# Key-value products on column halves: keys and values of an attention pair in blocks of 128 successive tokens

## The chip, the cores and the metric

The kernel runs on one core of a Trainium2 chip. The metric is the device time of one execution in microseconds (us); lower is better. All data are float32.

## The reference

Performer attention (random features in place of the softmax over keys) is followed by an FNet block (a Fourier transform as the mixer, then an MLP). There are 8 batches of 8 heads, 576 tokens, head dimension 64 and 128 random features.

```python
def phi(x):                                   # x = q or k, times 64**-0.25
    proj = np.einsum('bhsd,md->bhsm', x, omega)
    h = proj - np.sum(x * x, -1, keepdims=True) / 2
    h = h - np.max(h, -1, keepdims=True)
    return np.exp(h) / np.sqrt(m)
kv  = np.einsum('bhsm,bhsd->bhmd', phi(k), v)  # a sum over the tokens s
z   = np.sum(phi(k), axis=2)
num = np.einsum('bhsm,bhmd->bhsd', phi(q), kv)
den = np.einsum('bhsm,bhm->bhs', phi(q), z)[..., None] + 1e-6
x   = (num / den), heads side by side: (8, 576, 512)
mixed = real(fft(fft(x, tokens), channels)); u = x + mixed
un = layer_norm(u); out = u + relu(un @ w_ch1) @ w_ch2
```

The sums `kv` and `z` run over all tokens of a head, so the order of the tokens in them is free, as long as keys and values have the same one.

## The kernel before

A *pair* is two heads of one batch; there are 32 of them. The 1152 tokens of a pair (head 0's 576, then head 1's) lie on 128 partitions in R = 9 blocks. Before the change, partition p of each half of the tile holds the nine successive tokens 9p to 9p + 8 of one head, so in every block the partitions 0 to 63 are head 0 and 64 to 127 head 1.

`loads` fetches k and q of a pair into one tile `kq` (two buffers; lines L471 and L474), `load_v` the values into one of three tiles `vd` (L479), where each block has 64 columns of v and a 65th of ones, which makes `z` come out beside `kv`. All of these are issued by SP's queue, in a fixed order with the loads of the weights, the tables and the stores.

`attn` then does, for each pair: transposes of `kq` on TensorE (L607) and their copies out of PSUM (L621, L623); projections onto the features (L701, for the first six pairs on row halves, 64*128, for the others on quarters of the array, 64*64); the maximum (L644) and the exponential (L661) of softmax into tiles `e`; the **key-value step** (L735), which sums features times values over the nine blocks into two PSUM banks `kvp`; a copy of it to `kv` (L749 on VectorE or L751 on ScalarE); transposes of the query features (L607 again); the numerator and denominator (L782 and L790) on column halves, 128*64; and the division (L799 to L811).

The key-value step has four quarters: head i is rows 64i to 64i + 63 of the array, feature half h is its columns 64h to 64h + 63. Each head sums into its own bank, `kvp[cols, i]`. Each of the nine blocks gives one matmul to each quarter, 36 in all.

Beside the attention run the Fourier transforms of the batches that are done (L894, L904, L944, L955), conversions of the weights on DVE, ACT and POOL (L532 to L550), and the first token tiles of the MLP (L1236, L1259). The second part, from about 375 us on, is the rest of the MLP (L1727, L1878, L2178).

The order of instructions on each engine is fixed. A planner (`Listing`) takes the `Step`s of all streams, with a cost for each, and the picks of an earlier search are written into the kernel as strings; so the order of the work on each engine does not depend on what the steps really cost. The tile framework puts in the waits.

Of the kernel before, what the change touches and what calls it, by code (L numbers as in the profile page):

```python
# [375 lines left out]
def kernel(  # L376
# [10 lines left out]
    nc = tc.nc  # L387

    B, H, S, D = q.shape
# [13 lines left out]
    P = 128  # L403

    R = S // 64

    NS = 3
    NV = 3
# [38 lines left out]
        kq=NKQ, turned=NS, e=NE, e1=NS, kv=NS, x0=1, x1=1, fold=1, half=1, y=1,  # L447
# [8 lines left out]
    def got():  # L456

        return listing.got, psum_of(listing.got)
# [2 lines left out]
    kqs = {}  # L461
    vds = []

    def loads():
        for n in range(B * NP):
            b, pr = divmod(n, NP)
            h = slice(2 * pr, 2 * pr + 2)
            rows = "i (p r) d -> (i p) r d"
            yield Step(SP, 0.37, 3.0, take=("kq",), makes=("k", n), kb=288)
            kq = ld.tile([P, 2 * R, D], F32, name="kq", tag="kq")  # L470
            nc.sync.dma_start(kq[:, 0:R, :], k[b, h].rearrange(rows, r=R))  # L471
            kqs[n] = kq
            yield Step(SP, 0.47, 3.6, makes=("kq", n), kb=288, bias=-2.98)
            nc.sync.dma_start(kq[:, R : 2 * R, :], q[b, h].rearrange(rows, r=R))  # L474

    def load_v(n):
        b, pr = divmod(n, NP)
        yield Step(SP, 0.63, 4.0, take=(f"vd{n % NV}",), makes=("vd", n), kb=500, bias=0.52)
        nc.sync.dma_start(  # L479
            vds[n % NV][:, :, 0:D],  # L480
            v[b, 2 * pr : 2 * pr + 2].rearrange("i (p r) d -> (i p) r d", r=R),
        )

    def loads_v():
        for n in range(B * NP):
            yield from load_v(n)
# [181 lines left out]
    def attn(n):  # L668
        b, pr = divmod(n, NP)

        yield Step(NONE, after=(("k", n),) + ((("vd", n - 1),) if n else ()))
        kq = kqs.pop(n)
# [40 lines left out]
        def place(c):  # L713
            if c in (R - 1, R):
                return 2, c - (R - 1)
            return (c % 2, c // 2) if c < R else (3 + c % 2, (c - R - 1) // 2)

        def feature(c):
            t, i = place(c)
            return es[t][:, i, :]  # L720
# [8 lines left out]
            give=("e", "e", f"vd{n % NV}"), bias=-0.19,  # L729
        )  # L730
        kvb, kvp = got()
        for r in range(R):
            for i, h in ((0, 0), (1, 1), (0, 1), (1, 0)):
                rows, cols = slice(D * i, D * i + D), slice(D * h, D * h + D)
                nc.tensor.matmul(  # L735
                    kvp[cols, i, 0 : D + 1],
                    lhsT=feature(r)[rows, cols],
                    rhs=vds[n % NV][rows, r, :],
                    start=(r == 0),
                    stop=(r == R - 1),  # L740
                )
        kvs = []

        def keep():
# [32 lines left out]
        for i in range(2):  # L777
            for c in range(4):
                half = int(c in (1, 2))
                for g in range(2):  # L780
# [3 lines left out]
                        lhsT=flat[:, c0 : c0 + D],  # L784
                        rhs=kvs[0][:, i, :],
                    )

        for i in range(2):
            for g in range(2):
                nc.tensor.matmul(  # L790
                    ndp[D * g : D * g + D, i, (D + 1) * 4 : (D + 1) * 5],
                    lhsT=qeT[:, 0, D * i : D * i + D],
                    rhs=kvs[0][:, i, :],
# [775 lines left out]
    def pairs(start):  # L1569
        for n in range(start, B * NP, NS):  # L1570
            yield from attn(n)
# [45 lines left out]
    def betweens(text):  # L1617
# [6 lines left out]
    listing = Listing(buffers)  # L1624
    listing.run(
        [first(), loads(), loads_v(), load_tables(), frames(), plain_norms(), mixing()]
        + [pairs(i) for i in range(NS)]
        + [w2_parts(), weight_sums(), block_norms(0, mlpp), plain(), weights(), warm()],
# [766 lines left out]
```

## Time and profile before

| | |
|---|---|
| time, median of 3 runs | 1123.8 us (1123.35 to 1124.15) |
| span of the profiled execution, first to last instruction | 1119.2 us (its time as a whole is not listed apart; the median of the runs is 4.6 us more than its span) |
| TensorE (PE) busy | 1108.4 us, 99% |
| VectorE (DVE) busy | 888.7 us, 79% |
| ScalarE (ACT) busy | 539.5 us, 48% |
| GpSimd (POOL) busy | 390.6 us, 35% |
| key-value step, L735 | 41.5 us, 2304 records, between 10 and 355 us |
| numerator, L782 and L790 | 36.8 and 13.1 us |

A line of the profile names the source line, the engine, the operation, the tile written and the tiles read; for a matmul the part of the array in rows*columns (64*64 is a quarter, 128*64 a column half), then the moving operand. An fp32 matmul leaves two records. Times in the timeline are microseconds from the first instruction.

### The profile page before, as it was taken

To read this page: it belongs to the slowest core of one execution; us is meant where nothing else is said; L and a number is where in the kernel's file an instruction comes from. 1 tells how busy PE (TensorE), PEld (TensorE's weight loads), DVE (VectorE), ACT (ScalarE), POOL (GpSimd) and SP (SyncE) were. 2 spreads that over 40 slices of the span, in tenths; PEclk is the share of its full clock that TensorE was granted. 3 is DMA by queue.
4 is the path that set the end of the run, shared out by engine and by line. 5 is a ranking of instruction groups with operands and counts; after the bars stand their busy time and mean duration, and the time that the engine had idled before them with its cause. 6 is when DMAs were issued, how large, how long until landed. Compare 5 with 4: busy or idle time off the path is not lost.

```text
span 1119.2 us, 31666 instructions
## 1 busy us (share of the span) xinstructions
PE 1108.4 (99%) x12467; PEld 1000.4 (89%) x12467; DVE 888.7 (79%) x1685; ACT 539.5 (48%) x1644; POOL 390.6 (35%) x401
## 2 busy tenths in 40 slices
PE   9999999999999999999999999999999999999998
PEld 7888888879868778999999889999889999889998
DVE  6999999987576767687697777888677888568895
ACT  7998898856536455623214452223463223331221
POOL 2443443553563348634413464000365000152000
PEclk9999999999999999999999999999999999999999
DMA  8856766665674669798896778747678656546453
GB/s 243 243 174 188 242 180 191 183 208 176 216 232 156 194 172 343 224 314 262 260 326 224 226 216 248 207 148 238 206 207 261 207 155 216 170 152 220 146 160 105
DMA packets 196549, 236.13 MB, mean 211 GB/s; under 512 B 53808, under 2 KB 120624, under 8 KB 196400
## 3 DMA queue, kind: packets, MB, share of 16 engines
q1 hardware_dynamic: 195904, 233.83, 68.1%
q8 instruction: 99, 1.62, 0.6%
q14 instruction: 50, 0.41, 0.1%
q10 hardware_dynamic: 496, 0.26, 0.1%
HBM read 182.13 MB, written 56.10 MB: 213 GB/s over the span
## 4 chain that ended last, share of the span: by engine, by line
PE 92%; DVE 3%; ACT 2%; DMA 2%; issue 0%; POOL 0%; SPq 0%; DVEq 0%; ACTq 0%
PE banks L2178 31%; PE banks L1727 27%; PE banks L1236 5%; PE banks L701 5%; PE banks L607 5%; PE banks L1259 5%; PE banks L1878 4%; PE banks L735 3%; PE banks L782 2%; PE banks L944 2%; PE banks L894 1%; ACT e L661 1%; DVE nmx L644 1%; PE banks L904 1%; DMA unw<-turned 1%; DMA raw<-in_moe_w_ch_dram 1%
## 5 line engine op out<-in xcount | busy, mean ns | idle before, releaser
L2178 PE MATMUL banks<-wl,sums 128*128 128x128 f32 x1792 | 219.8, 275 | 0.0
L2178 PEld LDWEIGHTS banks<-wl,sums 128*128 128x128 f32 x1792 | 210.6, 192 | 1.0 <-issue 0.3
L661 ACT ACTIVATE e<-banks,nmx 128x128 f32<-128x128 f32 x576 | 165.7, 441 | 23.3 <-DVE nmx L644 22.9
L644 DVE TENSOR_REDUCE nmx<-banks 128x8 f32<-128x1024 f32 (+1 forms) x96 | 89.3, 951 | 16.8 <-PE banks L701 12.4
L2178 PE MATMUL banks<-wl,hid 128*128 128x128 f32 x768 | 99.2, 275 | 0.3 <-DVE part L2154 0.3
L2178 PEld LDWEIGHTS banks<-wl,hid 128*128 128x128 f32 x768 | 92.8, 192 | 1.2 <-DVE part L2154 0.8
L2149 ACT ACTIVATE s<-banks 128x128 f32<-128x128 f32 x112 | 30.9, 277 | 113.6 <-PE banks L2178 103.5
L1727 PE MATMUL banks<-unw,wxw 128*128 128x256 f32 x352 | 85.4, 379 | 0.0
L701 PE MATMUL banks<-om,kqT 64*64 64x128 f32 (+1 forms) x2088 | 79.0, 275 | 1.7 <-ACT kv L751 1.3
L701 PEld LDWEIGHTS banks<-om,kqT 64*64 64x64 f32 (+1 forms) x2088 | 64.5, 138 | 12.7 <-issue 3.2
L2178 PE MATMUL banks<-wl,hx 128*128 128x128 f32 x576 | 74.2, 275 | 0.4 <-DVE part L2154 0.4
L1727 PEld LDWEIGHTS banks<-unw,wxw 128*128 128x128 f32 x352 | 66.6, 190 | 8.9
L1727 PE MATMUL banks<-rx,wxw 128*128 128x256 f32 x288 | 70.8, 379 | 0.0
L2178 PEld LDWEIGHTS banks<-wl,hx 128*128 128x128 f32 x576 | 69.4, 192 | 0.8 <-DVE part L2154 0.6
L1752 ACT ACTIVATE s<-banks 128x512 f32<-128x512 f32 x65 | 38.5, 596 | 65.1 <-PE banks L1727 60.0
L1727 PE MATMUL banks<-ttw,wxw 128*128 128x256 f32 x288 | 69.8, 379 | 0.0
L1236 PE MATMUL banks<-unT,w 128*128 128x128 f32 x512 | 65.4, 279 | 1.7 <-DVE qeT L621 1.7
L550 POOL TENSOR_TENSOR w<-w,raw 128x512 f32<-128x512 f32 x28 | 37.6, 1351 | 77.3 <-DVE raw L544 68.1
L2227 POOL TENSOR_TENSOR more<-more,part 128x512 f32<-128x512 f32 x2 | 2.6, 1315 | 176.6 <-ACT part L2220 176.6
L1236 PEld LDWEIGHTS banks<-unT,w 128*128 128x128 f32 x512 | 60.2, 192 | 4.5 <-issue 2.3
L1727 PEld LDWEIGHTS banks<-rx,wxw 128*128 128x128 f32 x288 | 54.5, 190 | 7.3
L1727 PEld LDWEIGHTS banks<-ttw,wxw 128*128 128x128 f32 x288 | 54.5, 190 | 7.3
(287 smaller groups left out, 2442.3 us busy)
## 6 DMA issues: line engine op xcount, KB each, us to landing
wl<-w2l SPq DMA_DIRECT2D x245, 256.0 KB, 3.9
wxw<-w1x SPq DMA_DIRECT2D x120, 256.0 KB, 3.1
raw<-in_moe_w_ch_dram SPq DMA_DIRECT2D x32, 512.0 KB, 4.8
kq<-in_k_dram SPq DMA_DIRECT2D x32, 288.0 KB, 4.5
kq<-in_q_dram SPq DMA_DIRECT2D x32, 288.0 KB, 4.5
vd<-in_v_dram SPq DMA_DIRECT2D x32, 288.0 KB, 5.4
ur<-us SPq DMA_DIRECT2D x30, 256.0 KB, 5.2
w2l<-sums SPq DMA_DIRECT2D x14, 512.0 KB, 4.9
```

The costliest lines, as they stand in the source:

```text
L550: eng.tensor_tensor(out=dst, in0=dst, in1=lof, op=ALU.add)
L607: nc.tensor.transpose(ps[:, (j - j0) * 128 : (j - j0 + 1) * 128], src(j), ident[:])
L644: nc.vector.tensor_reduce(nmx[:, :, 0:num], pps[:, :, 0 : MF * num].rearrange("p b (c m) -> p b c m", m=MF), axis=AX.X, op=ALU.max, negate ...
L661: nc.scalar.activation(out=e[:, c + (i if num == 1 else 0), :], in_=pps[:, i, MF * c : MF * c + MF], func=AF.Exp, bias=nmx[:, i, c : c + 1],)
L701: nc.tensor.matmul(pps[cols, c, MF * m : MF * m + MF], lhsT=kqT[rows, j, cols], rhs=om2[rows, :],)
L735: nc.tensor.matmul(kvp[cols, i, 0 : D + 1], lhsT=feature(r)[rows, cols], rhs=vds[n % NV][rows, r, :], start=(r == 0), stop=(r == R - 1),)
L1236: nc.tensor.matmul(hp[:, 0:TP], lhsT=w1[:, dc, 128 * fc : 128 * fc + 128], rhs=unTs[key][:, dc, :], start=(dc == 0), stop=(dc == NDC - 1),)
L1259: nc.tensor.matmul(yp[:, 0:DM], lhsT=hs[fc][:, 128 * i : 128 * i + 128], rhs=w2[:, fc, :], start=(fc == 0), stop=(fc == NFC - 1),)
L1727: nc.tensor.matmul(ps[:, span * f : span * f + span].rearrange("f (b q) -> f b q", q=Q), lhsT=left[:, P * f : P * f + P], rhs=right, start ...
L1752: nc.scalar.activation(out=s[:], in_=ps, func=AF.Copy)
L1878: nc.tensor.matmul(cell.rearrange("f t (b q) -> f t b q", q=Q), lhsT=w[:, d, col : col + 128], rhs=right[:, :, d].rearrange("f (t b) q -> ...
L2178: nc.tensor.matmul(ps[:, 0:128], lhsT=left[:, f], rhs=wls[head(j), i, n][:, f], start=start and f == 0, stop=(f == 3), skip_group_check=True,)
```

## The change

Keys and values are laid out in blocks of 128 successive tokens: partition p of block r holds token 128r + p of the pair's 1152. Blocks 0 to 3 are then head 0 alone, blocks 5 to 8 head 1 alone, and block 4 has head 0 on partitions 0 to 63 and head 1 on 64 to 127. Queries keep their layout.

In the key-value step the middle block comes first, with four matmuls on quarters; every other block gives two matmuls of 128 rows, one on each column half, into its head's bank. This makes 4 + 8 x 2 = 20 matmuls per pair where 36 were. The order of the steps on every engine is as it was, and so are the planner's costs. The line of the key-value matmuls is L742 after the change, since seven lines are added above and in it.

```diff
+    def across(src):
+
+        return src.rearrange("i s d -> (i s) d").rearrange("(r p) d -> p r d", r=R)
+
     def loads():
...
-            nc.sync.dma_start(kq[:, 0:R, :], k[b, h].rearrange(rows, r=R))
+            nc.sync.dma_start(kq[:, 0:R, :], across(k[b, h]))
...
         nc.sync.dma_start(
             vds[n % NV][:, :, 0:D],
-            v[b, 2 * pr : 2 * pr + 2].rearrange("i (p r) d -> (i p) r d", r=R),
+            across(v[b, 2 * pr : 2 * pr + 2]),
         )
...
         kvb, kvp = got()
-        for r in range(R):
-            for i, h in ((0, 0), (1, 1), (0, 1), (1, 0)):
-                rows, cols = slice(D * i, D * i + D), slice(D * h, D * h + D)
-                nc.tensor.matmul(
-                    kvp[cols, i, 0 : D + 1],
-                    lhsT=feature(r)[rows, cols],
-                    rhs=vds[n % NV][rows, r, :],
-                    start=(r == 0),
-                    stop=(r == R - 1),
-                )
+        mid = R // 2
+        for r in (mid, *range(mid), *range(mid + 1, R)):
+            for i in range(2) if r == mid else (int(r > mid),):
+                rows = slice(D * i, D * i + D) if r == mid else slice(0, P)
+                for h in (i, 1 - i):
+                    cols = slice(D * h, D * h + D)
+                    nc.tensor.matmul(
+                        kvp[cols, i, 0 : D + 1],
+                        lhsT=feature(r)[rows, cols],
+                        rhs=vds[n % NV][rows, r, :],
+                        start=(r == mid),
+                        stop=(r == (mid - 1, R - 1)[i]),
+                    )
```

## The prediction

> **What bounds the kernel now.** I read the page first (engines, slices, chain), then busy time by stage, then the chain of waits in two stretches.
>
> ```profile
> span 1119.2 us, 31666 instructions
> PE 1108.4 (99%) x12467; PEld 1000.4 (89%) x12467; DVE 888.7 (79%) x1685; ACT 539.5 (48%) x1644; POOL 390.6 (35%) x401
> PE   9999999999999999999999999999999999999998
> PE 92%; DVE 3%; ACT 2%; DMA 2%; issue 0%; POOL 0%; SPq 0%; DVEq 0%; ACTq 0%
> ```
>
> TensorE (PE) has work in every slice, and 92% of the chain that ended last is its own. But the edited step lies in the first third, so I look there. The next rows give busy time in two stretches, then that of the edited line L735 alone in the same two, then the chain's shares in them.
>
> ```profile
> 0.00:125.00 125.00, 120.38 (x2555) 102.30 (x2559) 112.06 (x236) 108.77 (x391) 48.04 (x54) 1.00 0.74 218
> 125.00:375.00 250.00, 248.14 (x4709) 207.13 (x4699) 203.94 (x448) 168.76 (x601) 123.24 (x124) 1.00 0.63 196
> ...
> 0.00:125.00 125.00, 17.58 (x928) 15.69 (x932) 1.00 0.74 218
> 125.00:375.00 250.00, 23.88 (x1392) 22.32 (x1381) 1.00 0.63 196
> ...
> by line: PE banks L701 14.2%; ACT e L661 11.7%; PE banks L607 10.1%; DVE nmx L644 7.6%; DMA raw<-in_moe_w_ch_dram 7.1%; PE banks L735 6.8%; issue 3.8%; PE banks L944 3.5%; ACT qeT L623 2.6%; PE banks L578 2.3%; DVE w L539 2.0%; PE banks L89
> by line: PE banks L1236 16.9%; PE banks L701 16.2%; PE banks L607 15.9%; PE banks L1259 13.4%; PE banks L735 8.6%; PE banks L782 8.6%; PE banks L944 4.9%; PE banks L894 4.2%; PE banks L904 2.7%; PE banks L955 2.3%; PE banks L790 2.0%; DVE h
> ```
>
> In the row for 0 to 125 us PE, DVE and ACT are busy 120, 112 and 109 of 125 us: three engines near their limit, and the chain changes between them (ACT's L661 has 11.7% of it, DVE's L644 7.6%, a weight load 7.1%). L735 holds 6.8% of 125, or 8.5 us of it, against 17.6 us of busy time: about half its steps there decide anything. From 125 to 375 us PE is busy 248 of 250, and L735 has 8.6% of the chain, 21.5 us of its 23.9: there every step counts in full.
>
> **The key-value step itself.** First the two lines as the view of one line gives them, then places in PE's timeline (start, length, line, shape, count).
>
> ```profile
> L735 PE MATMUL banks<-vd,e x2304: 213/218/268, 10.4 to 354.8; 64*64 64x65 f32 x192
> L782 PE MATMUL banks<-kv,qeT x1024: 219/222/272, 18.5 to 371.7; 128*64 128x65 f32 x171
> ...
> 128.73 0.40 PE L790 MATMUL banks<-kv,qeT 128*64 128x65 f32 x7
> 129.06 1.28 PE L735 MATMUL banks<-vd,e 64*64 64x65 f32 x72
> 130.27 0.98 PE L607 MATMUL banks<-ident,e 128*128 128x128 f32 x7
> ...
> 150.91 1.28 PE L735 MATMUL banks<-vd,e 64*64 64x65 f32 x72
> 152.12 0.33 PE L607 MATMUL banks<-ident,e 128*128 128x128 f32 x1
> ...
> 154.21 1.10 PE L701 MATMUL banks<-om,kqT 64*64 64x128 f32 x32
> 155.13 1.23 PE L735 MATMUL banks<-vd,e 64*64 64x65 f32 x72
> 156.29 0.33 PE L607 MATMUL banks<-ident,e 128*128 128x128 f32 x1
> ...
> 161.34 1.15 PE L782 MATMUL banks<-kv,qeT 128*64 128x65 f32 x32
> 162.33 0.40 PE L790 MATMUL banks<-kv,qeT 128*64 128x65 f32 x8
> 162.56 1.10 PE L782 MATMUL banks<-kv,qeT 128*64 128x65 f32 x32
> 163.49 0.40 PE L790 MATMUL banks<-kv,qeT 128*64 128x65 f32 x8
> 163.73 0.28 PE L944 MATMUL banks<-cd_sb,y 128*64 128x129 f32 x1
> ...
> 83.29 1.28 PE L735 MATMUL banks<-vd,e 64*64 64x65 f32 x72
> 84.39 0.40 PE L701 MATMUL banks<-om,kqT 64*64 64x128 f32 x8
> ...
> 351.74 1.16 PE L701 MATMUL banks<-om,kqT 64*64 64x128 f32 x36
> 352.72 2.28 PE L735 MATMUL banks<-vd,e 64*64 64x65 f32 x144
> 354.93 0.82 PE L1236 MATMUL banks<-unT,w 128*128 128x128 f32 x5
> ```
>
> 2304 records are 32 pairs by 36 matmuls by two: each fp32 matmul is recorded twice. A step costs the time from its first start to the next step's first start.
>
> *Work.* The step at 155.13 takes 1.16 us; it follows matmuls of its own shape (64*64, quarters) and is followed by another shape. The two steps back to back from 352.72, after the quarters of L701, take 2.21, so the first, with quarters on both sides, takes 2.21 - 1.16 = 1.05 us for 36 matmuls. The numerator (L782 and L790) is 20 matmuls on column halves (128*64), 65 columns each, the form that the new key-value matmuls get. Between steps of its own shape it takes 163.73 - 162.56 = 1.17 us, or 0.0585 each. So the change's 16 halves cost 16 x 0.0585 = 0.94 us, and its 4 quarters a ninth of the old step, 0.12. Sum 1.05 us: exactly the old price. Twenty instructions do the work of 36 in the same time: each uses twice the rows, and half as many run side by side.
>
> *Shape changes.* The same rows price a change of shape. Leaving to another shape costs 1.16 - 1.05 = 0.11. Entering from another shape (150.91, after 64*128) makes the step 1.21 instead of 1.16, 0.05 more; L782 shows the same 0.05 (1.22 from 161.34, 1.17 from 162.56). Together 0.16 us for each change. The new step has a change that the old one had not, from the quarters of the middle block to the halves: +0.16 each. It also ends on halves. Nine of the 32 old steps were followed by quarters (the first at 83.29 takes 1.10 to the next line, the last of them is the first of the two at 352.72); each such exit becomes a change, +0.16. The entrance is as before, since the quarters come first. No row has quarters directly ahead of halves. The nearest is the reverse: at 129.06 quarters follow the halves of L790 and the step takes 1.21, as after any foreign shape. So I take 0.16; the bounds are 0 (halves and quarters share 64 columns, and no drain is needed in this direction) and 0.16 plus 0.06 to 0.12, one or two matmul slots, if the four quarters, now issued in the order (0,0), (0,1), (1,1), (1,0) instead of (0,0), (1,1), (0,1), (1,0), do not all run side by side. A gain here is excluded: the work is equal and no old change of shape goes. The Trainium skill, page "TensorEngine Tiling (Array Packing)", section "Key Properties", says that changing the tiling mode, not just the tile, drains TensorE. It gives no price and speaks for a change in this direction too, which no row shows; by it the sum stays at 0.16 each.
>
> *What counts.* From 125 us on 19 steps start, and half of the 13 before that, 7, are on the chain: 26 x 0.16 = 4.2 us. Of the nine exits I leave out those at 83 and 89 us, where ACT's part of the chain is widest: 7 x 0.16 = 1.1 us. If all 32 and 9 counted it would be 41 x 0.16 = 6.6 us; if only those after 125 us, 19 x 0.16 + 6 x 0.16 = 4.0.
>
> No wait is added: the middle block, which now opens the step, lies in the same softmax tile as block 0 did. Behind the longer step on PE's queue stand transposes and projections, and the copies L749/L751 start 0.16 later; the numerator is queued further back.
>
> **The loads.** K's load is cut into runs of 256 B where 2304 B were; v's was 256 B on the tile side already, and only its source addresses change. q is untouched.
>
> ```profile
> kq<-in_k_dram SPq DMA_DIRECT2D x32, 288.0 KB, 4.5
> kq<-in_q_dram SPq DMA_DIRECT2D x32, 288.0 KB, 4.5
> vd<-in_v_dram SPq DMA_DIRECT2D x32, 288.0 KB, 5.4
> ...
> 0.72 0.40 SPq L471 DMA_DIRECT2D kq<-in_k_dram  x1
> 2.59 1.53 SPq L479 DMA_DIRECT2D vd<-in_v_dram  x2
> 3.84 0.81 PE L607 MATMUL banks<-ident,kq 128*128 128x128 f32 x4
> ...
> PEld banks L607 <- DMA kq<-in_q_dram: 0.4, 2, 0.2
> ```
>
> V is the nearest row for the new k: 5.4 us to landing against 4.5, so +0.9, of which some is SP's longer issue (0.77 each against 0.40). The first transposes at 3.84 wait for the first k, issued at 0.72: nothing hides that load, and the start slips by between 0.4 (the issue alone) and 0.9. I take 0.7. Later loads are ahead of their use: in the whole run PE waits 0.4 us in two places on a DMA into kq. Behind each k on SP's queue stand q, v, the weights and the stores, each 0.37 later; with DMA engines busy 0.74 of the time in the first stretch that can cost up to 1.5 us, and at best nothing. Seeking v in other places is bounded by 0 and the same 1.5; I take 0 for both, since the one wait row is 0.4.
>
> **Sum.** 4.2 + 1.1 + 0.7 = 6.0 us on the profiled span of 1119.2. The median of the runs, 1123.8, lies 4.6 above that span; launch and end are not touched. Forecast 1123.8 + 6.0 = 1129.8 us, or +0.5%.
>
> **Rivals.** *The changes of shape are free or absorbed.* Then only the start is left, 0.7, perhaps with the 0.05 inside: 1124.5 to 1126. For it: halves and quarters share their columns, and ACT and DVE have waits of PE to fill before 125 us. Against: 129.06, and 19 steps with no idle time around them. Chance 0.08, all within 0.2% (2.2 us, about what a measurement of this kernel can tell from no change).
>
> *The step is bound by the number of its instructions* (faster). Its place is the same step; it decides if the 72 records, 1.05/72 = 0.0146 us apart, are PE's fastest issue. Then 40 records take 0.58, each step gains 0.47 and loses 0.16, and 26 x 0.31 = 8.1 less 1.1 and 0.7 gives 1123.8 - 6.3 = 1117.5. Against it stands the numerator: 40 records took 1.17 us at 128*64, 0.029 apart, so the stream of columns sets the pace. Chance 0.05. The Trainium skill, page "TensorE: Matmul & The Clock Gate", section "Wait — 56ns, not 53.3ns?", speaks for this rival: starts never come closer than about 25 ns, however few the columns. By it 72 records would need 1.8 us and 40 would need 1.0, an estimate. This trace disagrees: 0.0146 us between starts.
>
> *Short runs hurt more than v shows* (slower still). K and v together crowd the queue in the first stretch, and the weight load, 7.1% of the chain there, comes later: the upper bounds 1.5 + 1.5, with all 41 changes, 6.6, and the start, 0.7, give 1134. It decides once PE's waits on DMA rows exceed 1 us. Chance 0.12. With the quarters in series (26 x 0.06 to 0.12 = 1.6 to 3.1) it is as far; chance 0.05, 1131.4 to 1133.
>
> **The numbers.** Forecast with its spread 0.70. Range: down to 1126.0 (after-125 changes at 0.11, 25 x 0.11 = 2.8, with little of the start), up to 1134.0. Faster 0.05; same 0.08; slower 0.87.
>
> **What would show it.** PE's timeline after: the step's line has 1280 records in two shapes, 8 of 64*64 and 32 of 128*64 each time, and lasts 1.32 to 1.37 us to another shape, never less than 1.2. Its busy time rises by about 5 us while its records fall from 2304. K lands in about 5.4 us, the first transposes begin at about 4.5. From 125 to 375 us the same work ends some 4 us later in addition. After that nothing moves: the MLP's stretches have the same lengths. The forecast is wrong if the step takes 1.05 to 1.2, if the halves follow the quarters without a gap, or if PE's idle time shrinks by as much as the steps grow.

## The result and the profile after

| kernel | median of the runs, us | ratio to before, 95% interval |
|---|---|---|
| before | 1123.8 | |
| after | 1128.5 (1126.3 to 1129.6) | 1.0043 (1.0027 to 1.0059) |

The change makes the kernel slower by 4.8 us (3.0 to 6.6). The forecast was 6.0 slower, 1129.8 us in a range of 1126.0 to 1134.0.

From the page of after: the span and the instructions, the busy time of the engines, and the chain that ended last, by engine.

```profile
span 1126.7 us, 29618 instructions
PE 1113.4 (99%) x11443; PEld 1003.0 (89%) x11443; DVE 887.9 (79%) x1685; ACT 539.9 (48%) x1644; POOL 389.6 (35%) x401
PE 90%; DVE 3%; ACT 3%; DMA 2%; SPq 1%; issue 1%; POOL 0%; DVEq 0%; POOLq 0%; ACTq 0%
```

PE's records fall by 1024 and its busy time rises by 5.0 us, from 1108.4. The traced run of after took 1128.5, 1.8 more than its span; the 4.6 that I took for before was therefore not launch and end alone: its traced run must have been one of about 1121.0, 2.8 under the median. So a span of another kernel set against 1119.2 shows some 2.8 more than the medians do (7.5 here).

Where the time went is read by finding the same event in both traces. The reciprocal in each pair's division is such an event; here are the twelfth and the last of the 32, of before and then of after (start, length).

```profile
130.19 0.22 DVE L800 RECIPROCAL rden<-rden 128x10 f32<-128x10 f32 x1
373.02 0.22 DVE L800 RECIPROCAL rden<-rden 128x10 f32<-128x10 f32 x1
```
```profile
133.65 0.22 DVE L807 RECIPROCAL rden<-rden 128x10 f32<-128x10 f32 x1
380.53 0.22 DVE L807 RECIPROCAL rden<-rden 128x10 f32<-128x10 f32 x1
```

After is 3.5 us late at the twelfth, 7.5 at the last, and still 7.5 at the end of the span: the MLP's part, two thirds of the run, does not move. So before's stretches 0 to 125 and 125 to 375 us hold the work of 0 to 128.5 and 128.5 to 382.5 us of after. Busy time in these (bounds, length, then PE, PEld, DVE, ACT, POOL, clock, DMA share, GB/s):

```profile
0.00:128.50 128.50, 121.57 (x2143) 102.86 (x2145) 113.34 (x236) 109.21 (x392) 48.05 (x54) 1.00 0.81 212
128.50:382.50 254.00, 252.00 (x4089) 209.17 (x4085) 203.34 (x448) 168.79 (x601) 123.06 (x124) 1.00 0.65 192
```

Against before, the second stretch is 4.0 us longer and PE 3.9 us busier, with 2.0 us idle where 1.9 were: nearly all of it is longer matmul work. Behind the idle time stand a new wait of 0.6 us on ScalarE at 171 us and one that shrank by 0.3, below. The first is 3.5 longer, but PE only 1.2 busier (121.57 against 120.38); the other 2.3 are idle time, and the DMA share went from 0.74 to 0.81. That points to two causes, one in each stretch.

The step itself, first by its line, then in PE's timeline: entered from another shape (154.61), entered from quarters (158.98), and left to quarters (263.65).

```profile
L742 PE MATMUL banks<-vd,e x1280: 217/222/272, 10.7 to 362.3; 128*64 128x65 f32 x146, 64*64 64x65 f32 x37
154.61 1.43 PE L742 MATMUL banks<-vd,e 64*64 64x65 f32 x40
155.97 0.33 PE L611 MATMUL banks<-ident,e 128*128 128x128 f32 x1
...
158.98 1.38 PE L742 MATMUL banks<-vd,e 64*64 64x65 f32 x40
160.29 0.33 PE L611 MATMUL banks<-ident,e 128*128 128x128 f32 x1
...
263.65 1.38 PE L742 MATMUL banks<-vd,e 64*64 64x65 f32 x40
264.96 1.10 PE L705 MATMUL banks<-om,kqT 64*64 64x128 f32 x32
265.99 0.76 PE L611 MATMUL banks<-ident,e 128*128 128x128 f32 x5
```

The step at 154.61 is before's at 150.91: 1.36 us to the next line where 1.21 were. That at 158.98 is before's at 155.13: 1.31 where 1.16 were. So the change of shape inside costs 0.15, predicted as 0.16. The step at 263.65 is before's at 257.50, here with what follows it:

```profile
257.50 1.23 PE L735 MATMUL banks<-vd,e 64*64 64x65 f32 x72
258.54 1.05 PE L701 MATMUL banks<-om,kqT 64*64 64x128 f32 x32
259.53 0.77 PE L607 MATMUL banks<-ident,e 128*128 128x128 f32 x5
```

It had 1.04 to L701 and has 1.31 now, and L701 itself 0.99, now 1.03: 0.15 for the change inside and 0.16 (0.12 and 0.04) for the exit to quarters, as predicted. The Trainium skill, page "TensorEngine Tiling (Array Packing)", section "Key Properties", says that a change of tiling mode drains TensorE; the trace fits it, in this direction too: a change costs 0.15 to 0.16 us.

### The profile page after: what moved, and what is told of

It is laid out like the page before. It is cut to its first block, busy times and chain, and to the rows that moved or that the text cites. A ratio compares the mean times of both kernels' runs of the same rounds, so it can differ in the third digit from the quotient of the medians.

```text
span 1126.7 us, 29618 instructions
## 1 busy us (share of the span) xinstructions
PE 1113.4 (99%) x11443; PEld 1003.0 (89%) x11443; DVE 887.9 (79%) x1685; ACT 539.9 (48%) x1644; POOL 389.6 (35%) x401
## 4 chain that ended last, share of the span: by engine, by line
PE 90%; DVE 3%; ACT 3%; DMA 2%; SPq 1%; issue 1%; POOL 0%; DVEq 0%; POOLq 0%; ACTq 0%
PE banks L2185 31%; PE banks L1734 27%; PE banks L1243 5%; PE banks L705 5%; PE banks L1266 5%; PE banks L611 4%; PE banks L1885 4%; PE banks L742 3%; PE banks L789 2%; DMA raw<-in_moe_w_ch_dram 2%; PE banks L951 1%; PE banks L901 1%; ACT e L665 1%; PE banks L911 1%; SPq L520 1%; DVE nmx L648 1%
```

## Experiments

My theory after the comparison: in the second stretch the changes of shape, in the first the loads. The rival: that the first stretch, too, is the step's, and the loads cost next to nothing. The first four runs part them. Differences in us are the ratio less one, times before's 1123.

**The loads alone**: layout of after, step of before.

```diff
+    def across(src):
+        return src.rearrange("i s d -> (i s) d").rearrange("(r p) d -> p r d", r=R)
...
-            nc.sync.dma_start(kq[:, 0:R, :], k[b, h].rearrange(rows, r=R))
+            nc.sync.dma_start(kq[:, 0:R, :], across(k[b, h]))
...
-            v[b, 2 * pr : 2 * pr + 2].rearrange("i (p r) d -> (i p) r d", r=R),
+            across(v[b, 2 * pr : 2 * pr + 2]),
```

> The new loads of k and v with the old key-value step (36 quarters), so that the heads' tokens are mixed in the sums. Theory of shapes (each added change of the array's shape costs 0.16 us, loads little): the first transposes start at about 4.3 us as in the changed kernel, +0.4 to +1.0 us in all, 1124.2 to 1124.8; from 125 to 375 us no further slip. Rival, the loads: short runs delay the weight loads of the first stretch, where the changed kernel had already lost 3.4 of its 7.5 us by 130 us; then +2.5 to +3.5 us, 1126.3 to 1127.3, nearly all before 130 us.

Measured: 1126.4 us, ratio 1.0027 (1.0015 to 1.0039), 3.0 us slower, as the rival had it; "loads little" is refuted.

**The step alone**: step of after, loads of before (the keys and values of a block then belong to two heads, so the products mix them). Against after:

```diff
-            nc.sync.dma_start(kq[:, 0:R, :], across(k[b, h]))
+            nc.sync.dma_start(kq[:, 0:R, :], k[b, h].rearrange(rows, r=R))
...
-            across(v[b, 2 * pr : 2 * pr + 2]),
+            v[b, 2 * pr : 2 * pr + 2].rearrange("i (p r) d -> (i p) r d", r=R),
```

> The old loads with the new key-value step (4 quarters, 16 halves); heads are mixed in the sums. Theory of shapes: +4.0 us of slip between 125 and 375 us (25 changes of 0.16) and 1 to 1.5 before, in all +5.0 to +5.5, 1128.8 to 1129.3. Rival, the loads: no more than +1 to +2 us, 1124.8 to 1125.8.

Measured: 1125.5 us, 1.0021 (1.0011 to 1.0031), 2.4 slower, where 5.0 to 5.5 were expected and the rival had 1 to 2. Its trace is 5.0 us over before's, but that trace is of a run 2.8 under before's median, as said above. The stretches that hold the same work, of the loads alone and then of the step alone:

```profile
0.00:127.80 127.80, 119.75 (x2555) 102.42 (x2559) 112.29 (x236) 108.95 (x391) 47.97 (x54) 1.00 0.81 213
127.80:378.10 250.30, 248.12 (x4709) 207.14 (x4699) 203.94 (x448) 168.55 (x601) 123.04 (x124) 1.00 0.67 196
```
```profile
0.00:126.75 126.75, 121.72 (x2141) 102.73 (x2143) 112.37 (x236) 108.68 (x391) 47.90 (x54) 1.00 0.75 215
126.75:380.00 253.25, 251.87 (x4091) 209.23 (x4086) 203.93 (x448) 168.19 (x601) 122.92 (x124) 1.00 0.63 193
```

The loads cost 2.8 us in the first stretch, all of it idle time of PE, and 0.3 in the second. The step costs 1.8 in the first and 3.3 in the second, nearly all of it busy time. That parts the two causes. In the second stretch the measured prices make 19 x 0.15 + 6 x 0.16 = 3.8. The traces show where 0.3 of the missing 0.5 went: the step near 314 us stands ahead of PE's one long wait there, the first row here from before, the second from after.

```profile
PE banks L1236 <- DVE qeT L621: 1.7, 1, 1.7
```
```profile
PE banks L1243 <- DVE qeT L625: 1.4, 1, 1.4
```

That wait, 1.4 in the step alone too, shrinks by the 0.3 of its step and exit: a change of shape in front of a wait is absorbed. So 3.5 are left, and after's 4.1 are these and the 0.6 of its new wait on ScalarE, which the traces of the step alone and of after again don't have.

**Without the quarters**: the middle block, too, on halves. It leaves the separation of the two heads in that block out.

```diff
-        for r in (mid, *range(mid), *range(mid + 1, R)):
-            for i in range(2) if r == mid else (int(r > mid),):
-                rows = slice(D * i, D * i + D) if r == mid else slice(0, P)
+        for r in range(R):
+            i = int(r > mid)
...
```

> The changed kernel with the middle block taken as one of head 0's: 18 matmuls on halves, no quarters, left out is the middle block's share in head 1's sum. The stream of columns is as long as before (18 slots of 0.0585). Theory of shapes: the change inside the step is gone; entrances from quarters become changes (10 after 125 us), entrances from the numerator are free (2), exits to quarters cost (5 after 125 us): 13 x 0.16 = 2.1 us of slip between 125 and 375 us where the changed kernel had 4.1; about 1126.5. Rival, halves are slower in themselves (twice the rows, accumulation into the same place at each slot): the slip between 125 and 375 us stays at about 4, 1128.5.

**The quarters in the middle**, so that each step has two changes of shape inside.

```diff
-        for r in (mid, *range(mid), *range(mid + 1, R)):
+        for r in range(R):
...
-                        start=(r == mid),
-                        stop=(r == (mid - 1, R - 1)[i]),
+                        start=(r == (0, mid)[i]),
+                        stop=(r == (mid, R - 1)[i]),
```

> The changed kernel with the middle block in its natural place, between head 0's four blocks and head 1's: the same 20 matmuls, two changes of shape inside each step instead of one. Theory of shapes: between 125 and 375 us 38 changes inside, 8 more entrances and 5 exits, 51 x 0.16 = 8.2 us of slip against before where the changed kernel had 4.1; in all 1132.5 to 1134.5. Rival, the number and kind of matmuls or the loads: the same as the changed kernel, 1128.5.

Measured: without the quarters 1126.8 us, 1.0031 (1.0019 to 1.0042); in the middle 1132.9, 1.0085 (1.0070 to 1.0100). The step that was at 150.91 in before, without the quarters and then with them in the middle:

```profile
156.74 1.27 PE L741 MATMUL banks<-vd,e 128*64 128x65 f32 x36
157.94 0.33 PE L611 MATMUL banks<-ident,e 128*128 128x128 f32 x1
```
```profile
156.23 1.58 PE L742 MATMUL banks<-vd,e 128*64 128x65 f32 x40
157.74 0.33 PE L611 MATMUL banks<-ident,e 128*128 128x128 f32 x1
```

1.20 with no change of shape inside, 1.36 in after with one, 1.51 with two: each adds 0.15 to 0.16. Work and number of matmuls are the same in the last two, so it is the change that costs. From the twelfth reciprocal to the last the two kernels lost 1.6 and 7.0 us, where the theory had 2.1 and 8.2: somewhat less, as with the step alone. What the kernel without the quarters lost besides, it lost in the first stretch: its trace is 6.1 us late at the twelfth reciprocal, and 3.1 of that are two waits for loads of `kq` (below).

**Which load, and when.** K's runs alone; v's addresses alone; and k's short runs only from the 13th pair on, with v as before. (`across` is added as above.)

```diff
# k alone / k late
-            nc.sync.dma_start(kq[:, 0:R, :], k[b, h].rearrange(rows, r=R))
+            nc.sync.dma_start(kq[:, 0:R, :], across(k[b, h]))
+            nc.sync.dma_start(kq[:, 0:R, :], across(k[b, h]) if n >= 12 else k[b, h].rearrange(rows, r=R))
# v alone
-            v[b, 2 * pr : 2 * pr + 2].rearrange("i (p r) d -> (i p) r d", r=R),
+            across(v[b, 2 * pr : 2 * pr + 2]),
```

> The old kernel with k's load alone in the new layout (runs of 256 B); v's load and the step are old, so keys and values do not belong together in the sums. With both loads the time rose by 3.0 us, and PE stood 1.4 us at 82 us for the q of one pair, whose landing had 0.14 us to spare before. Theory of short runs: k is the cause, k_alone rises by 2 to 3 us over before and that q is late again. Rival, v's scattered addresses: k_alone rises by no more than the start's 0.4 to 0.7 us.

> The old kernel with v's load alone from the new places (its runs were 256 B on the tile side before and stay so); keys and values do not belong together in the sums. Theory of short runs: within 0.5 us of before. Rival, v's scattered addresses: +2 to 3 us, with that q late.

> The old kernel with k's load in 256 B runs for the pairs from 12 on (issued after 95 us), the first twelve as before; keys and values of those 20 pairs do not belong together in the sums. With all 32 k loads so the time rose by 2.6 us. Theory: what costs is the first stretch, where three engines and the loads are at their limit (the first load, and the q that has 0.14 us to spare at 81 us); then this kernel is within 0.8 us of before. Rival, every short load costs alike (more traffic for the rest): 20/32 of 2.6, +1.6 us.

Measured: k alone 1126.5 us, 1.0026 (1.0013 to 1.0038), 2.9 slower; v alone 1123.9, 0.9998 (0.9987 to 1.0008); k late 1123.7, 1.0015 (0.9999 to 1.0030), at most 3.4. So the loads' cost is k's short runs, and v's addresses cost nothing that is clear of noise. In the trace of k late the twelfth reciprocal comes 0.4 us earlier than in before: the early cost is gone with the early runs. Its time doesn't settle what the later runs cost: 1.7 us by the ratio (-0.1 to 3.4) is the rival's 1.6, 0.4 by the medians is the theory's, and in its trace the work from the twelfth reciprocal to the last takes 3.8 us longer, of which 2.4 are gaps of a kind that is treated under the count of matmuls. How k's runs delay the work is read from SP's issues in the first 90 us (min/median/max ns), here of before, k alone, the loads alone and after, in this order; in v alone and k late q's median is 433 and 432 ns:

```profile
L474 SPq DMA_DIRECT2D kq<-in_q_dram x12: 421/432/1460, 1.2 to 82.9; - x12
```
```profile
L478 SPq DMA_DIRECT2D kq<-in_q_dram x12: 422/814/3714, 1.2 to 86.4; - x12
```
```profile
L475 SPq DMA_DIRECT2D kq<-in_k_dram x12: 368/403/1218, 0.7 to 85.2; - x12
L478 SPq DMA_DIRECT2D kq<-in_q_dram x12: 422/1046/3469, 1.2 to 85.8; - x12
```
```profile
L478 SPq DMA_DIRECT2D kq<-in_q_dram x12: 422/918/2294, 1.2 to 85.8; - x12
```

K's own issue hardly changes (0.40 us at the median, 0.37 in before), but q's, the next behind it on SP, takes 0.8 to 1.0 instead of 0.43, and only where the k ahead of it has short runs. Q's own descriptors are the same in all of these. So it is held up behind k's, and with it what stands behind on SP; what in the queue holds it up, no run here shows. One q that this makes late is that of the 11th pair. SP's timeline around it, in before and with the loads alone:

```profile
72.84 0.33 SPq L471 DMA_DIRECT2D kq<-in_k_dram  x1
73.23 0.59 SPq L479 DMA_DIRECT2D vd<-in_v_dram  x1
75.25 0.98 SPq L564 DMA_DIRECT2D raw<-in_moe_w_ch_dram  x1
76.27 0.43 SPq L474 DMA_DIRECT2D kq<-in_q_dram  x1
```
```profile
73.81 0.38 SPq L475 DMA_DIRECT2D kq<-in_k_dram  x1
74.25 3.06 SPq L483 DMA_DIRECT2D vd<-in_v_dram  x1
77.43 1.08 SPq L568 DMA_DIRECT2D raw<-in_moe_w_ch_dram  x1
78.55 1.57 SPq L478 DMA_DIRECT2D kq<-in_q_dram  x1
```

In before this q is issued by 76.70, lands at 81.19 and is first read at 81.32: 0.13 us to spare (landing and reading from the trace's records). With the loads alone v's issue, just behind k's, takes 3.06 us instead of 0.59 and q is issued by 80.12. PE waits for it, in six of the seven traces with k's first runs short: here the loads alone and after again (the changed kernel once more, below). K alone has 1.6, without the quarters 2.7, the quarters in the middle and the best placing (below) 1.4 each.

```profile
PE banks L611 <- DMA kq<-in_q_dram: 1.4, 1, 1.4
```
```profile
PE banks L611 <- DMA kq<-in_q_dram: 1.1, 1, 1.1
```

None of the seven traces with k's first runs long has such a wait. After's first trace doesn't have it either: there 0.3 us go to k, and the rest comes by ScalarE, whose kv PE waits for 2.0 us in all where before had 1.3. The longest of these waits, 1.4 us, is the queue's doing too. SP and ScalarE in after:

```profile
33.97 4.45 SPq L520 DMA_DIRECT2D cd_sb<-k_cd  x2
40.73 0.37 SPq L568 DMA_DIRECT2D raw<-in_moe_w_ch_dram  x1
...
45.50 0.68 ACT L538 ACTIVATE w<-raw 128x512 f32<-128x512 f32 x1 [1.17 <-DMA raw<-in_moe_w_ch_dram]
46.08 0.26 ACT L758 ACTIVATE kv<-banks 128x130 f32<-128x130 f32 x1
```

In before the two issues of the table `cd_sb` take 1.60 us, and the load of MLP weights (`raw`) behind it and the next table starts at 36.19. Here it starts at 40.73, ScalarE stands 1.17 us for it, and the copy of kv behind it comes late. After again has the same (41.16, 0.92 us of waiting, 1.1 for kv); the loads alone doesn't (38.14, no such wait).

**The change again, and on row halves.** After was run again beside these kernels: 1129.1 us, 1.0047 (1.0034 to 1.0060).

> The changed kernel beside the others, for its interval on the same chip and a second trace. If the slip after 130 us comes from shapes alone it is again 4.1 us from there to 375 us, while what is lost before 130 us differs from run to run; +4.5 to +5.5 us over before. If the loads act in the later stretch too, the later slip differs from 4.1 by more than 1 us.

The other kernel takes the old layout and puts six pairs' key-value steps on row halves, 64 rows by 128 columns, 18 matmuls each: six that follow matmuls on row halves, so that a change of shape at their start goes.

```diff
+ROWS = (0, 2, 3, 4, 14, 17)
...
-            for i, h in ((0, 0), (1, 1), (0, 1), (1, 0)):
-                rows, cols = slice(D * i, D * i + D), slice(D * h, D * h + D)
+            for i, h in ((0, 0), (1, 0)) if n in ROWS else ((0, 0), (1, 1), (0, 1), (1, 0)):
+                rows, cols = slice(D * i, D * i + D), slice(D * h, P if n in ROWS else D * h + D)
```

> The old kernel, old loads, with the key-value step of six pairs (those that follow work on row halves: four of the first five, and those at about 151 and 183 us) on row halves, 64*128, 18 matmuls instead of 36; same sums. Theory of shapes: six entrances and two exits are no changes any more, 8 x 0.16 = 1.3 us less of PE's time, of which the two after 125 us (0.3 us) count in full and the others where PE ends the waits: 1122 to 1122.9 with before at 1123.0. Rival: on row halves the two heads do not run side by side, each of the six steps takes 2.1 instead of 1.05 us: +2 to +6 us.

Measured: 1132.3 us, 1.0068 (1.0054 to 1.0081), 7.6 slower: the theory's gain did not come. The same step of before and of this kernel (35.49 and 35.39), each with the line behind it:

```profile
35.49 1.28 PE L735 MATMUL banks<-vd,e 64*64 64x65 f32 x72
36.70 0.77 PE L607 MATMUL banks<-ident,e 128*128 128x128 f32 x5
```
```profile
35.39 2.12 PE L736 MATMUL banks<-vd,e 64*128 64x65 f32 x36
37.45 0.77 PE L608 MATMUL banks<-ident,e 128*128 128x128 f32 x5
```

It takes 2.06 us where 1.21 were; six times the difference is 5.1 of the 7.6; the rest is not worked out. That is the rival's time, but not for its reason: in the trace's records the two heads' matmuls start 0.007 us apart, so they do run side by side, and one such pair follows the other after 0.11 us. The projections on row halves, 64*128 too, keep the same 0.11 with 128 moving columns (before, from 34.40), where column halves with 65 take 0.0585. So on row halves the pace is not set by the moving columns. A weight load of this form has 128 columns, and its longest record is 189 ns against 135 for 64 columns: I take it that the weight loads set the pace, but no run here varies them alone.

**The best placing of the one change.** In six steps the quarters go last: where the step is followed by quarters, the exit then costs nothing, and where it follows the numerator's halves, the entrance.

```diff
+LAST = (11, 13, 15, 19, 28, 31)
...
+        last = n in LAST
+        order = (*range(mid), *range(mid + 1, R), mid) if last else (mid, *range(mid), *range(mid + 1, R))
...
```

> The changed kernel with the middle block last instead of first in six pairs: the two that follow the numerator's halves, the three that are followed by quarters and not preceded by them, and the second of the two back to back. Same matmuls, same sums, six changes of shape fewer, all after 124 us. Theory of shapes: 6 x 0.15 = 0.9 us less slip between 125 and 375 us (2.4 to 3.2 where the changed kernel had 3.3 to 4.1), in all 1.0048 x before less 0.9, 1127.5 to 1128.5 with before at 1123.5. Rival, the place of the middle block doesn't matter: as the changed kernel, 1128.5 to 1129.

Measured: 1127.0 us, 1.0037 (1.0023 to 1.0050). From the twelfth reciprocal to the last it loses 2.5 us, where after's two runs lost 4.1 and 3.2. It is the fastest form with all its products that I found, but its interval overlaps after's, so that it beats after is shown by the steps in the trace and not by the time. It is still 4.2 us slower than before; no complete version beats before.

**The count of matmuls.** Before once more, for its trace, and before with 22 of its 36 matmuls on quarters; the others are left out.

> The old kernel once more, for a second trace: if the loss before 130 us differs from run to run, its first 130 us of work end up to 2 us later than in the first trace, and everything after 130 us lasts the same to within 0.3 us. Otherwise both traces agree to 0.3 us throughout.

```diff
-            for i, h in ((0, 0), (1, 1), (0, 1), (1, 0)):
+            for i, h in ((0, 0), (1, 1), (0, 1), (1, 0)) if r in (0, R - 1) else ((0, 0), (1, 1)) if r % 2 else ((0, 1), (1, 0)):
```

> Old kernel, old loads, old quarters, but only 22 of the 36 key-value matmuls: blocks 0 and 8 give all four, odd blocks only (0,0) and (1,1), even ones only (0,1) and (1,0); the rest of each block's products is left out. Two questions. First, TensorE's gaps that end with 'issue': the kernels with 36 matmuls a step had 0 to 4.4 us of them in the profile, mostly near the steps at 17-18 and 128-140 us, those with 20 had none. Theory of supply (the number of instructions makes them): none here, as in the kernels with 20. Rival (the quarters or the old place make them): 0.4 to 3 us of them remain. Second, what a step is worth: the quarter with most has 6 of 9 matmuls, so the pure step goes from 1.05 to about 0.70 us, 0.35 less. If steps after 125 us count in full and half of the earlier ones, as predicted, 26 x 0.35 = 9 us faster, 6.6 of it between 125 and 375 us; if the steps' length were hidden in part, less than 6.

Measured: before again 1122.3 us (one run, span 1120.5). Both forms of what I expected of it miss: the twelfth reciprocal is only 0.3 us later than in the first trace, but from there to the last it takes 1.1 us longer, so a slip between two traces is known here to no better than that. With 22 matmuls 1116.6, 0.9946 (0.9929 to 0.9962), 6.1 faster, where 9 were expected. The stretches of the latter with before's work:

```profile
0.00:127.00 127.00, 118.64 (x2209) 100.49 (x2213) 112.67 (x236) 108.01 (x391) 47.59 (x54) 0.99 0.74 214
127.00:370.80 243.80, 242.44 (x4153) 200.11 (x4145) 202.19 (x448) 168.06 (x601) 124.13 (x124) 1.00 0.65 201
```

The second stretch is 6.2 us shorter, with 6.6 expected, and PE's busy time in it 5.7: there a step is worth nearly its full length in both directions. The first is 2.0 longer, though 13 steps in it lost 0.35 each: PE now waits for ScalarE's qeT, once, at 77 us:

```profile
PE banks L782 <- ACT qeT L623: 2.2, 1, 2.2
```

Half of each early gain was expected, and none came. Before 125 us a shorter step buys nothing in this trace.

A gap of PE that the view ends with "issue" is one in which PE waited for nothing that the view shows. The longest such row of before again:

```profile
PE banks L735 <- issue: 1.3, 1, 1.3
```

Six of the seven traces of kernels with 36 matmuls a step (six row-half steps in one of them) have 0.4 to 4.4 us of such gaps, most of them inside or near this step (k alone has none). None of the seven traces of kernels with 18 to 22 matmuls in every step has any.

The traces show more than the view does. Queue q8 brings instructions; first its row on before's page, then on after's (packets, MB, share):

```profile
q8 instruction: 99, 1.62, 0.6%
```
```profile
q8 instruction: 91, 1.49, 0.6%
```

After has 2048 instructions fewer, all of them PE's, and 8 packets fewer; with 22 matmuls it is 1792 and 7, without the quarters 2304 and 9. So q8 feeds PE, 256 instructions to a packet. By the trace's records all 19 "issue" gaps of the seven traces end 1.30 to 1.61 us after a packet of q8 has landed; of PE's 66 other waits in these traces (0 to 400 us) 4 do, the rest at anything from 0.1 to 9.6 us. So in these gaps PE waits for its instructions. It fits that the step is the place: 36 matmuls and their weight loads are 144 records in 1.05 us, so a packet is used up in some 1.9 us there, an estimate, while one takes 1.0 us to come (median) and PE goes on 1.3 us later at the earliest. Why k alone has no such gap is not shown.

## Why the prediction was right

**The price of a change of shape** (0.16): the step lasts 1.31 to 1.36 us to another shape, as forecast (1.32 to 1.37). It is 0.15 inside a step, 0.16 at an exit to quarters, measured on after, and doubled and taken away in two experiments. The bounds of 0 and of quarters in series are both refuted: eight records of the quarters start within 0.13 us.

**From 125 to 375 us, 4.0**: after 4.1, after again 3.2, the step alone 3.3. Right, to within the 1.1 us by which the two traces of before differ there. I overlooked the wait at 327 us (before's time), which absorbs 0.3; that after comes so near to 4.0 is in part its 0.6 us on ScalarE, which I had not foreseen.

**The steps before 125 us**, 7 of 13 and one exit, 1.3: 1.8 in the trace of the step alone. About right for a loss, and wrong for a gain, as the 22 matmuls show.

**The loads, 0.7**: this is the term that was mis-sized by its mechanism: the crowded queue behind k was set at nothing. Alone they cost 3.0 (1.7 to 4.4). The start was too high: K's first landing let the transposes begin at 4.28 where I expected 4.5, and over all its loads k lands in after in 4.5 us at the median, as fast as it did in before, not in 5.4.

What failed is the sentence that later loads are ahead of their use, taken from the one wait row of 0.4 us. A row of waits shows who is late now, not how near the others are; q of the 11th pair had 0.13 us to spare. The bound for what stands behind k on SP, 0 to 1.5, was of the right kind, and I took its lower end; even its upper end makes 1.9 with the start's 0.4. Nor did the price "0.37 later each", the rise of the issue itself, hold: the delay is in the issues behind it.

**The sum**: 6.0 against 4.8 (3.0 to 6.6), with two errors that offset, so that the total came so near is in part luck. The step alone was forecast at 5.3 and timed at 2.4 (1.2 to 3.5), the loads at 0.7 and timed at 3.0. The step's trace is 5.0 us over before's, as forecast; but that trace of before was of a run 2.8 under its median. Part of what before's other runs lose is in the waits for instructions that the kernels with 20 matmuls don't have: before again has 1.8 us more of them than the first trace. The longest, 1.3 at 18 us, cost it nothing; one at 139 us, 0.6 in the view, sets the work behind it back by 0.9 of the 1.3 us by which its span is longer. So the smaller count gives back something that no row of the one trace of before showed; that this makes up the whole 2 to 3 us is argued, not shown. The range's lower end is also not the sum that it names: 1123.8 + 2.8 is 1126.6, not 1126.0.

**The rivals.** Free or absorbed changes: refuted by the step's rows. A step bound by its instructions: refuted for the step itself, 40 records take as long as 72 did; the number counts by another way, the waits for instructions between. The Trainium skill, page "TensorE: Matmul & The Clock Gate", section "Wait — 56ns, not 53.3ns?", by which starts are never closer than about 25 ns, would have made it true; before's 72 records in 1.05 us and the eight quarter records within 0.13 us disagree. Short runs that hurt more: its mechanism, a crowded queue behind k, is what happened in the first stretch, and its condition, over 1 us of waits on DMA rows, held in the loads alone (1.8 in the first stretch) and after again (1.8), though not in after's first trace (0.3). The later weight load that I had named came as well, in both traces of after (40.73 and 41.16 for 36.19). But all of this together was worth 3.0 us and not 3.7, and it stood beside a step that was timed cheaper, so the whole stayed below the forecast.

## What to carry to other kernels

Count the places where the array's shape changes before counting matmuls: a new one cost as much as two to three matmuls of 65 columns, and halving the instructions at equal array time gained nothing in the step; what it removed are waits for instructions, which the view of waits shows without their cause. Before cutting a load into shorter runs, look at what is issued behind it on the same queue and at the smallest margin between landing and use, since a table of waits shows neither. Ahead of a wait, or where another engine is as full, a longer or shorter step can come out at nothing; test each stretch by itself.

## What was not expected

An issue on SP is lengthened more by the runs of the DMA ahead of it than by its own: q's from 0.43 to 0.8 to 1.0 us at the median, k's own from 0.37 to 0.40. A matmul on a row half with 65 moving columns keeps the array for longer than its columns would ask: 18 of them took 2.06 us where 36 on quarters took 1.21. And PE stood up to 1.3 us at a time within runs of 72 short records, waiting for its own instructions, in nearly every trace of kernels with 36 matmuls a step and in none of those with fewer in every step.
